# A long convolution with a routed expert layer on one core: the late units' transposes of finished rows move from behind a unit's first step to the unit's head

## The chip, the core and the metric

The kernel runs on one core of a Trainium2 chip. The metric is the time of one execution in microseconds, as the device measures it. The core has TensorE (PE: matrix products and transposes into PSUM; its weight loads are listed apart, as PEld), VectorE (DVE), ScalarE (ACT), GpSimd (POOL, which here also issues the DMAs that gather and scatter rows by a list of indices) and SyncE (SP, which issues plain DMAs). Each engine works through its own list of instructions in the order in which the program wrote them, and semaphores make one engine wait for another.

## The reference

Two layers follow one another. The first is a long convolution of `u = x * v` with a filter, done with Fourier transforms, and a product with `x`:

```python
u = x * v                                   # 4 x 11456 x 128
y = np.fft.irfft(Uf * Hf[None, :, :], n=L, axis=1)[:, :S, :]
return (x * y).astype(np.float32)
```

The second takes the 45,824 rows of that result. A row whose skip score is positive goes through the one of eight experts with the largest logit, and the result, times the expert's gate weight, is added to the row:

```python
h = np.maximum(xc[mask] @ w1[e], 0.0)       # 128 -> 1024
y[mask] = gate_w[mask, None] * (h @ w2[e])  # 1024 -> 128
out[do_compute] = xc + y
```

Rows with a score of zero or less are left as they are.

## The kernel before

The program has four stretches. `first_phase` and `freq_phase` (to about 730 us) compute the convolution's forward transforms and products, `out_phase` (to about 1183 us) transforms back, stores the rows, routes them and already runs a part of the experts' work in between (`early_slots`). What is left of the experts' work runs in `late_slots`, from about 1183 us to the end. The change lies in `late_slots` alone.

`late_slots` works through 36 *units*, `u` = 0 to 35. Units 0 to 28 hold two *slots* each and are called pairs here; units 29 to 31 hold one slot (singles), and units 32 to 35 half a slot (halves). A slot is 256 rows of one expert. For a pair, 512 rows go through these steps:

- **Gather.** `fetch(u + 4)` has POOL gather the rows of the unit four ahead into tiles `xt` (L666), with a short POOL pause behind them (L639).
- **Turning the rows.** `turned(sts(u + 1))` transposes the next unit's rows on PE, four 128x128 transposes (L718) into the PSUM tile `mtp`; ACT copies them to `hl` (L720) and DVE writes what the rounding lost beside it (L724).
- **Going up.** `up` multiplies with the expert's first weights, in four parts `k` = 0 to 3 of six matmuls each (L729 to L731) into a PSUM tile `hp`, of which there are two in turn. `relu` reads `hp` on ACT (L850) and then on DVE (L851) into `hh`.
- **Going down.** `down` multiplies `hh` with the second weights (L862 to L864). It is written as a generator, and `lower()` takes one quarter of it: while unit `u` goes up, the four quarters of unit `u - 1` go down, one behind each part. Behind the last quarter, ACT copies the PSUM tile `my` to `yt` (L868).
- **Turning the results back.** `leave(sts(u - 2), yt.pop(u - 2))` transposes the finished `yt` of the unit two back on PE, four transposes (L875) into the PSUM tile `mto`; DVE multiplies with the gate weight and adds the row (`gated`, L742), and POOL scatters the result into the output (L735), with a pause behind it. The program wraps it in a local function `finish()`.
- **Splitting weights.** `first` and `second` prepare the next unit's first weights and this unit's second ones (ACT L701, DVE L706).

The order is written out by hand, since the stretch is scheduled manually: what the loop over `u` writes first is first on each engine. At the head of a unit the loop writes `fetch` and `turned`. Then the four parts follow, each as `up`, `lower`, `relu` and one step more out of the list `(finish, first, second, nothing)`. So before the change `finish()`, with the transposes L875, stands behind part 0 of a pair. In a single it stands behind part 0 as well, in a half behind `lower()`.

The name `st` holds the gathered rows of each slot and `part(u)` says whether unit `u` is a half.

Of the kernel before, what the change touches and what calls it, by code (L numbers as in the profile page):

```python
# [487 lines left out]
class Experts:  # L488
# [149 lines left out]
    def rest(self):  # L638
        self.nc.gpsimd.memset(self.idle, 0.0)  # L639
# [185 lines left out]
    def late_slots(self, pool):  # L825
# [4 lines left out]
        with (  # L830
# [6 lines left out]
            def turned(sts):  # L837
                return self.turn(sts, pool, mpt.tile([128, 2 * T], F32, name="mtp"))

            def up(w, hl, part):  # L840
                n = hl.shape[2]
                hp = mph.tile([128, 4 * T], F32, name="hp")
                nf = 4 * T // n
                for f in range(nf):
                    self.up(w, hl, hp[:, f * n:(f + 1) * n], part * nf + f)
                return hp

            def relu(hp):
                h = mb.tile([128, 2, 4 * T], F32R, name="hh", bufs=6)
                nc.scalar.activation(h[:, 0], hp, AF.Relu)  # L850
                nc.vector.scalar_tensor_tensor(h[:, 1], hp, 0.0, h[:, 0].bitcast(F32), ALU.max, ALU.subtract)  # L851
                return h

            def down(w2, parts, n):

                y = mpy.tile([128, 2 * T], F32, name="my")[:, 0:n]
                nf = 4 * T // n
                for f in range(F // 128):
                    c = slice(f * D, (f + 1) * D)
                    k = f % nf  # L860
                    h = parts[f // nf][:, :, k * n:(k + 1) * n]
                    nc.tensor.matmul(y, w2[:, 0, c], h[:, 0], start=(f == 0), stop=False)  # L862
                    nc.tensor.matmul(y, w2[:, 0, c], h[:, 1], start=False, stop=False)
                    nc.tensor.matmul(y, w2[:, 1, c], h[:, 0], start=False, stop=(f == F // 128 - 1))  # L864
                    if k == nf - 1 and f < F // 128 - 1:
                        yield
                yt = mb.tile([128, 2 * T], F32, name="yt")[:, 0:n]
                nc.scalar.copy(yt, y)  # L868
                yield yt

            def leave(sts, yt):

                tp = mpt.tile([128, 2 * T], F32, name="mto")
                for j in range(2 * len(sts)):
                    nc.tensor.transpose(tp[:, j * 128:(j + 1) * 128], yt[:, j * 128:(j + 1) * 128], self.ident)  # L875
                for n, (tb, xt, ids, since) in enumerate(sts):
                    o = self.row()
                    for j in range(2):
                        self.gated(o[:, j, 0:D], tp[:, n * T + j * 128:n * T + (j + 1) * 128], xt, j)
                        self.store(o[:, j], ids, j)  # L880
                self.rest()

            def turned_half(st):
                tp = mpt.tile([128, 2 * T], F32, name="mtp")[:, 0:128]
                nc.tensor.transpose(tp, st[1][:, 0, 0:D], self.ident)
                x = pool.tile([128, 2, 2 * T], F32R, name="hl", bufs=2)[:, 0, 0:128].bitcast(F32)
                nc.scalar.copy(x, tp)
                return x

            def weight_half(st, which, p, eng):  # L890
                w = p.tile([128, 2, F], F32R, name=f"ws{which}", bufs=2)[:, 0].bitcast(F32)
                src = (self.w1f, self.w2f)[which][:, ds(self.where(eng, st[0]), F)]
                (eng.copy if eng is nc.scalar else eng.tensor_copy)(w, src)
                return w

            def up_half(w, x):
                hp = mph.tile([128, 4 * T], F32, name="hp")
                for f in range(F // 128):
                    c = slice(f * 128, (f + 1) * 128)
                    nc.tensor.matmul(hp[:, c], w[:, c], x, start=True, stop=True)  # L900
                h = mb.tile([128, 2, 4 * T], F32R, name="hh", bufs=6)[:, 0].bitcast(F32)
                nc.scalar.activation(h, hp, AF.Relu)
                return h

            def down_half(w, h):

                y = mpy.tile([128, 2 * T], F32, name="my")[:, 0:D]
                for f in range(F // 128):
                    c = slice(f * 128, (f + 1) * 128)
                    nc.tensor.matmul(y, h[:, c], w[:, c], start=(f == 0), stop=(f == F // 128 - 1))  # L910
                yield y

            def leave_half(st, y):
                tb, xt, ids, since = st
                o = self.row()
                self.gated(o[:, 0, 0:D], y, xt, 0)
                self.store(o[:, 0], ids, 0)
                self.rest()
# [6 lines left out]
            def fetch(u):  # L925
                if u < count:
                    for n in UNITS[u]:
                        if n not in st:
                            st[n] = self.gather(n, self.listing(n), pool, self.names[n])
                            if n == UNITS[u][-1]:  # L930
                                self.rest()
            for u in range(FETCH):
                fetch(u)
            sts = lambda u: [st[n] for n in UNITS[u]]
            part = lambda u: UNITS[u][0] >= HALF
            w2, yt = {}, {}
            before = iter(())
            for u in range(count + 2):
                fetch(u + FETCH)
                if u + 1 < count:  # L940
                    hl[u + 1] = turned_half(*sts(u + 1)) if part(u + 1) else turned(sts(u + 1))

                def first():
                    if u + 1 < count and part(u + 1):
                        w1[u + 1] = weight_half(*sts(u + 1), 0, pool, nc.scalar)
                    elif u + 1 < count:
                        w1[u + 1] = self.split(st[UNITS[u + 1][0]][0], pool, 0, nc.vector)

                def second():
                    w2[u] = self.split(st[UNITS[u][0]][0], mb, 1, nc.vector)  # L950

                def finish():
                    if u >= 2 and not part(u - 2):
                        leave(sts(u - 2), yt.pop(u - 2))

                def lower():
                    y = next(before, None)
                    if y is not None:
                        yt[u - 1] = y
                        if part(u - 1):  # L960
                            leave_half(*sts(u - 1), y)
                parts = []
                if u >= count:
                    lower()
                    finish()
                elif part(u):
                    w2[u] = weight_half(*sts(u), 1, mb, nc.vector)
                    first()
                    parts = up_half(w1[u], hl[u])
                    lower()  # L970
                    finish()
                elif len(UNITS[u]) == 1:
                    first()
                    hp = up(w1[u], hl[u], 0)
                    finish()
                    parts.append(relu(hp))
                    second()
                    parts.append(relu(up(w1[u], hl[u], 1)))
                else:
                    for k, rest in enumerate((finish, first, second, lambda: None)):  # L980
                        hp = up(w1[u], hl[u], k)
                        lower()
                        parts.append(relu(hp))
                        rest()
                while u >= 1 and u - 1 < count and u - 1 not in yt:
                    lower()
                if u < count:
                    before = down_half(w2[u], parts) if part(u) else down(w2[u], parts, hl[u].shape[2])
                    del w1[u], hl[u]
# [458 lines left out]
```

## Time and profile before

| | us |
|---|---|
| median of 3 timed runs | 1583.29 |
| lowest and highest of them | 1579.92, 1583.38 |
| the profiled execution's own time | 1577.83 |
| its span in the trace | 1576.1 |

The profile is of one execution. Its instructions are listed by engine with their start, their duration and, in square brackets, the time that the engine was idle before and which instruction ended that wait. A matmul's duration is modelled from its start to the last value that it writes, so that matmuls in a row overlap in the list: where they follow each other closely it is the distance between two starts that tells what one costs. Rows of one line that follow each other are merged into one, with "x4" for four. The program's names stand with the result on the left: `mto<-ident,yt` writes `mto` from `ident` and `yt`.

### The profile page before, as it was taken

The numbers are of one execution on the slowest core, as the hardware profiler recorded it, in microseconds if no ns is written. First come the engines' busy times: TensorE is split into PE (matmuls) and PEld (weight loads), VectorE is DVE, ScalarE is ACT, GpSimd is POOL, SyncE is SP. The second block draws the span as 40 slices with busy tenths as digits, with TensorE's granted clock in tenths as the row PEclk, the third lists the DMA queues.
The fourth block names the chain that finished last, engine by engine and source line by source line (L and its number), as shares of the span: only waits on it lengthen the run. The fifth ranks groups of instructions, "written<-read, shape, count | busy, mean of one in ns | idle before, by whom it ended". The sixth has DMA issues, their size and how long they took to land. (4 is left out here: it accounts for less than half of the span.)

```text
span 1576.1 us, 25413 instructions
## 1 busy us (share of the span) xinstructions
PE 1502.5 (95%) x7872; PEld 935.1 (59%) x7872; DVE 1127.8 (72%) x2323; ACT 767.3 (49%) x1637; POOL 1081.1 (69%) x832
## 2 busy tenths in 40 slices
PE   8995999999999999998889999999989999999998
PEld 3552444444444444443457777677767888888888
DVE  2334877888788889996777777776666777777774
ACT  4552545444444544442345554544535555555554
POOL 2013898888888878882166758865777888888756
PEclk9987999999999999998899999999999999999999
DMA  9999999999999979978988778878521111111100
GB/s 318 328 351 338 375 354 366 375 348 335 320 353 331 304 229 290 336 212 275 342 251 291 233 256 262 272 270 252 158 57 37 46 45 47 44 46 44 41 24 29
DMA packets 200382, 361.84 MB, mean 230 GB/s; under 512 B 64588, under 2 KB 140762, under 8 KB 200206
## 3 DMA queue, kind: packets, MB, share of 16 engines
q1 hardware_dynamic: 181078, 316.97, 59.3%
q0 software_dynamic: 16448, 38.88, 8.4%
q10 hardware_dynamic: 2720, 4.34, 0.9%
q8 instruction: 64, 1.05, 0.3%
q14 instruction: 72, 0.59, 0.1%
HBM read 216.70 MB, written 145.42 MB: 230 GB/s over the span
## 5 line engine op out<-in xcount | busy, mean ns | idle before, releaser
L411 PE MATMUL ps<-y,c 128*128 128x512 f32 x720 | 331.3, 596 | 0.3
L479 POOL TENSOR_TENSOR y<-y,p 128x2048 f32<-128x2048 f32 x59 | 267.8, 4540 | 69.0 <-DVE p L400 69.0
L735 POOL DMA_INDIRECT out<-o,ids x182 | 198.5, 1091 | 115.4 <-DVE o L742 77.9
L411 PEld LDWEIGHTS ps<-y,c 128*128 128x128 f32 x720 | 133.4, 190 | 173.0 <-issue 155.7
L666 POOL DMA_INDIRECT xt<-out,ids x182 | 192.5, 1058 | 57.0 <-issue 23.8
L400 DVE TENSOR_TENSOR p<-xp,g 128x1024 f32<-128x1024 f32 x240 | 217.3, 946 | 0.0
L400 DVE TENSOR_TENSOR y<-xp,g 128x1536 f32<-128x1536 f32 x120 | 210.8, 1757 | 4.0
L851 DVE SCALAR_TENSOR_TENSOR hh<-hp,hh 128x1024 fp32r<-128x1024 f32 x122 | 148.7, 1219 | 88.5 <-ACT hh L850 87.2
L412 ACT COPY z<-ps 128x512 f32<-128x512 f32 x180 | 105.6, 586 | 178.3 <-PE ps L411 168.8
L850 ACT ACTIVATE hh<-hp 128x1024 fp32r<-128x1024 f32 x122 | 126.4, 1036 | 88.3 <-PE hp L731 88.3
L480 POOL TENSOR_TENSOR y<-y,p 128x1024 f32<-128x1024 f32 x59 | 139.1, 2358 | 4.6
L1107 PE MATMUL y<-zt,c 128*64 128x512 f32 x384 | 110.8, 650 | 16.6 <-DVE xm L1108 5.1
L639 POOL MEMSET idle<- 128x512 f16 x231 | 126.3, 547 | 0.3
L380 PE MATMUL xp<-x,wf 128*128 128x480 f32 x256 | 115.6, 575 | 11.1 <-DMA x<-x1f 6.7
L209 PE MATMUL ps<-wf,c 60*120 60x384 f32 x512 | 110.9, 528 | 8.0 <-DVE wf L192 8.0
L211 ACT COPY wf<-ps 120x384 f32<-120x384 f32 x256 | 105.3, 493 | 21.2 <-PE ps L209 11.2
L812 PE MATMUL bank<-wd,h 128*128 128x128 f32 x896 | 115.0, 283 | 0.0
L812 PEld LDWEIGHTS bank<-wd,h 128*128 128x128 f32 x896 | 105.1, 193 | 14.6 <-issue 14.0
L192 POOL TENSOR_TENSOR wf<-wf 124x768 f32<-124x768 f32 x45 | 81.9, 1819 | 41.5 <-DVE g L392 31.2
L729 PE MATMUL hp<-hl,ws 128*128 128x512 f32 (+1 forms) x256 | 103.2, 403 | 2.1 <-DVE hh L851 1.4
L383 ACT COPY g<-xp 64x192 f32<-64x192 f32 x120 | 38.0, 316 | 137.4 <-PE xp L380 94.7
L392 DVE TENSOR_TENSOR g<-xp,g 128x128 f32<-128x128 f32 x120 | 34.7, 289 | 97.2 <-ACT g L385 97.0
(199 smaller groups left out, 2925.0 us busy)
## 6 DMA issues: line engine op xcount, KB each, us to landing
wf<-xv SPq DMA_DIRECT2D x64, 768.0 KB
x1d<-wf SPq DMA_DIRECT2D x64, 720.0 KB
x<-x1d SPq DMA_DIRECT2D x60, 768.0 KB
zt<-zd SPq DMA_DIRECT2D x60, 768.0 KB
zd<-z SPq DMA_DIRECT2D x110, 384.0 KB
out<-xm SPq DMA_DIRECT2D x96, 258.0 KB
ox<-xo SPq DMA_DIRECT2D x96, 256.0 KB
x1f<-fx POOLq DMA_DIRECT2D x16, 720.0 KB
```

The source lines that it names most:

```text
L209: nc.tensor.matmul(ps[p], self.c1[rows], u[rows, q * RUN:(q + 1) * RUN], start=True, stop=True)
L380: nc.tensor.matmul(xp[:, k, 0:(NS + NB) * DH], c2(n % PER * KS + j * KH + k), x1[:, j * KH + k], start=True, stop=True)
L400: nc.vector.tensor_tensor(o[:, :, :, j * KH:(j + 1) * KH].rearrange("p s a k b d -> p (s a) k b d"), x[:, None].broadcast_to([128, m, KH, ...
L411: nc.tensor.matmul(zps, c3[:, a, :], y[:, blk, a], start=(a == 0), stop=(a == 1))
L479: nc.gpsimd.tensor_tensor(y[:, 1:], y[:, 1:], p1, ALU.add)
L480: nc.gpsimd.tensor_tensor(y[:, 2:], y[:, 2:], p2, ALU.add)
L639: self.nc.gpsimd.memset(self.idle, 0.0)
L666: ins = nc.gpsimd.indirect_dma_start(out=xt[:, j], out_offset=None, in_=self.rows[0:have], in_offset=bass.IndirectOffsetOnAxis(ap=ids[:, j ...
L735: ins = nc.gpsimd.indirect_dma_start(out=self.rows, out_offset=bass.IndirectOffsetOnAxis(ap=ids[:, j:j + 1], axis=0), in_=o, in_offset=Non ...
L812: nc.tensor.matmul(bank[:, j * D:(j + 1) * D], h[f][:, j * 128:(j + 1) * 128], wd[s][:, f * D:(f + 1) * D], start=(f == 0), stop=(f == F / ...
L850: nc.scalar.activation(h[:, 0], hp, AF.Relu)
L851: nc.vector.scalar_tensor_tensor(h[:, 1], hp, 0.0, h[:, 0].bitcast(F32), ALU.max, ALU.subtract)
```

## The change

The turning back of unit `u - 2` is now written at the head of unit `u`, right behind the turning of unit `u + 1`'s rows. The function `finish` is gone, and what called it now calls nothing:

```diff
                 fetch(u + FETCH)
                 if u + 1 < count:
                     hl[u + 1] = turned_half(*sts(u + 1)) if part(u + 1) else turned(sts(u + 1))
+                if u >= 2 and not part(u - 2):
+                    leave(sts(u - 2), yt.pop(u - 2))
...
-                def finish():
-                    if u >= 2 and not part(u - 2):
-                        leave(sts(u - 2), yt.pop(u - 2))
...
                 if u >= count:
                     lower()
-                    finish()
                 elif part(u):
...
                     lower()
-                    finish()
                 elif len(UNITS[u]) == 1:
                     first()
                     hp = up(w1[u], hl[u], 0)
-                    finish()
                     parts.append(relu(hp))
...
-                    for k, rest in enumerate((finish, first, second, lambda: None)):
+                    for k, rest in enumerate((lambda: None, first, second, lambda: None)):
```

On PE, at the head of unit 3, the difference reads as follows ("+" is now, "-" is before; `mtp` is the turning of the next unit's rows, `mto` the turning back, `hp` part 0 going up):

```order
 L718 MATMUL mtp<-ident,xt_4453 128x128 x2
 L718 MATMUL mtp<-ident,xt_4454 128x128 x2
+L875 MATMUL mto<-ident,yt 128x128 x4
 L729 MATMUL hp<-hl,ws_13155 128x512
 L730 MATMUL hp<-hl,ws_13155 128x512
```

The four transposes of `yt` now stand between the turning of rows and part 0. Their place before, twelve matmuls on in the same unit, behind the first quarter going down (`my`) and ahead of part 1:

```order
 L863 MATMUL my<-hh,ws_13192 128x512
 L864 MATMUL my<-hh,ws_13192 128x512
-L875 MATMUL mto<-ident,yt 128x128 x4
 L729 MATMUL hp<-hl,ws_13155 128x512
 L730 MATMUL hp<-hl,ws_13155 128x512
```

So they moved up over the six matmuls of part 0 and the six of the quarter, to stand with the other four transposes. On PE nothing else moved.

On DVE, behind the writing of `hl` for the next unit, the four `gated` steps (L742) moved over one `relu` step (L851), that of part 0. The piece of the difference:

```order
 L655 COPY tb<-tab 1x1 x2
 L724 TENSOR_TENSOR hl<-mtp,hl 128x512
-L851 SCALAR_TENSOR_TENSOR hh<-hp,hh 128x1024
 L742 SCALAR_TENSOR_TENSOR o_4461<-mto,xt_4447 128x128 x2
 L742 SCALAR_TENSOR_TENSOR o_4458<-mto,xt_4448 128x128 x2
-L851 SCALAR_TENSOR_TENSOR hh<-hp,hh 128x1024
+L851 SCALAR_TENSOR_TENSOR hh<-hp,hh 128x1024 x2
```

So part 0's `relu` on DVE now stands behind the four `gated` steps, beside that of part 1. The order on ACT is the same as before. On POOL it is the same but for one place near the end, where the last single's two scatters now stand ahead of a half's one. No instruction is added or taken away on any engine.

## Rows read from the trace of the kernel before

**Rows 1.** Busy time by engine over the 27 periods from the head of unit 2 to the head of unit 29 (us, number of instructions in brackets, granted clock of TensorE as a share of full speed, DMA share and GB/s).

```profile
1209.23:1528.85 319.62, 319.62 (x1512) 264.20 (x1511) 237.40 (x347) 184.77 (x216) 247.25 (x257) 1.00 0.16 42
```

**Rows 2.** Groups of PE instructions by line in the same stretch: busy us, mean ns of one, and the idle time of PE before them.

```profile
L729 PE MATMUL hp<-hl,ws 128*128 128x512 f32 x216 | 89.1, 413 | 0.0
L718 PE MATMUL mtp<-ident,xt 128*128 128x128 f32 x107 | 16.2, 272 | 0.0
L875 PE MATMUL mto<-ident,yt 128*128 128x128 f32 x108 | 16.1, 272 | 0.0
```

**Rows 3.** The timeline of one pair, PE alone: its head, the place of the turning back, and the next unit's head (start us, duration us).

```profile
1303.79 0.39 PE L864 MATMUL my<-hh,ws 128*128 128x512 f32 x1
1304.02 0.60 PE L718 MATMUL mtp<-ident,xt 128*128 128x128 f32 x4
1304.37 0.48 PE L729 MATMUL hp<-hl,ws 128*128 128x512 f32 x1
1304.69 0.39 PE L730 MATMUL hp<-hl,ws 128*128 128x512 f32 x1
...
1306.97 0.40 PE L864 MATMUL my<-hh,ws 128*128 128x512 f32 x1
1307.20 0.60 PE L875 MATMUL mto<-ident,yt 128*128 128x128 f32 x4
1307.56 0.47 PE L729 MATMUL hp<-hl,ws 128*128 128x512 f32 x1
1307.87 0.40 PE L730 MATMUL hp<-hl,ws 128*128 128x512 f32 x1
...
1310.40 0.39 PE L729 MATMUL hp<-hl,ws 128*128 128x512 f32 x1
...
1315.62 0.40 PE L864 MATMUL my<-hh,ws 128*128 128x512 f32 x1
1315.85 0.60 PE L718 MATMUL mtp<-ident,xt 128*128 128x128 f32 x4
```

**Rows 4.** The same unit's timeline, ACT and DVE.

```profile
1304.22 0.59 ACT L868 COPY yt<-my 128x512 f32<-128x512 f32 x1 [2.12 <-PE my L864]
1304.70 1.03 ACT L850 ACTIVATE hh<-hp 128x1024 fp32r<-128x1024 f32 x1
1305.77 1.23 DVE L851 SCALAR_TENSOR_TENSOR hh<-hp,hh 128x1024 fp32r<-128x1024 f32 x1 [2.22 <-ACT hh L850]
1307.03 0.67 DVE L724 TENSOR_TENSOR hl<-mtp,hl 128x512 fp32r<-128x512 f32 x1
1307.63 1.20 DVE L851 SCALAR_TENSOR_TENSOR hh<-hp,hh 128x1024 fp32r<-128x1024 f32 x1
1308.76 1.11 DVE L742 SCALAR_TENSOR_TENSOR o<-mto,xt 128x128 f32<-128x128 f32 x4
```

**Rows 5.** The timeline at the end of `out_phase`, at one of the 18 places where the weight load of a first transpose (PEld L718) waited for ACT L755.

```profile
1181.90 1.30 ACT L755 ACTIVATE h<-mh 128x512 f32<-128x512 f32 x2 [0.41 <-PE mh L731]
1182.55 0.42 PEld L718 LDWEIGHTS mh<-ident,xt 128*128 128x128 f32 x4 [0.47 <-ACT h L755]
1182.93 1.20 PEld L812 LDWEIGHTS bank<-wd,h 128*128 128x128 f32 x10
1183.04 1.17 PE L812 MATMUL bank<-wd,h 128*128 128x128 f32 x9
```

**Rows 6.** The timeline at unit 29, the first single: PE's wait behind its part 0.

```profile
1531.87 0.39 PE L729 MATMUL hp<-hl,ws 128*128 128x256 f32 x1 [0.76 <-DVE tb L655]
```

**Rows 7.** The timeline at the heads of units 30, 31, 32 and 33, PE and ACT.

```profile
1539.22 0.28 PE L730 MATMUL hp<-hl,ws 128*128 128x256 f32 x1
1539.08 0.59 ACT L868 COPY yt<-my 128x512 f32<-128x512 f32 x1 [4.44 <-PE my L864]
...
1545.51 0.28 PE L730 MATMUL hp<-hl,ws 128*128 128x256 f32 x1
1545.54 0.37 ACT L868 COPY yt<-my 128x256 f32<-128x256 f32 x1 [1.74 <-PE my L864]
...
1551.46 0.94 PE L900 MATMUL hp<-hl,ws 128*128 128x128 f32 x7
1551.89 0.37 ACT L868 COPY yt<-my 128x256 f32<-128x256 f32 x1 [1.76 <-PE mtp L885]
...
1556.45 0.72 PE L900 MATMUL hp<-hl,ws 128*128 128x128 f32 x5
1556.59 0.37 ACT L868 COPY yt<-my 128x256 f32<-128x256 f32 x1 [1.89 <-PE my L864]
```

**Rows 8.** Waits from 1190 to 1530 us: who waited for whom, us in total, times, longest.

```profile
POOL out L735 <- DVE o L742: 22.7, 27, 5.8
```

**Rows 9.** Busy time by stretches (columns as in rows 1), for the granted clock.

```profile
800.00:880.00 80.00, 74.17 (x678) 54.52 (x679) 57.28 (x208) 39.75 (x95) 52.14 (x59) 0.96 0.78 251
880.00:960.00 80.00, 78.61 (x721) 58.51 (x719) 61.05 (x233) 40.59 (x101) 53.59 (x61) 1.00 0.85 270
1040.00:1120.00 80.00, 78.19 (x677) 54.73 (x675) 57.58 (x223) 38.44 (x98) 51.17 (x60) 1.00 0.79 247
1532.00:1560.00 28.00, 28.00 (x217) 26.99 (x218) 18.00 (x29) 16.83 (x23) 18.01 (x20) 1.00 0.11 34
```

**Rows 10.** The timeline of the end: the last matmuls, the last `gated` step and the last scatter.

```profile
1565.70 3.74 PE L910 MATMUL my<-ws,hh 128*128 128x128 f32 x32
1569.48 0.35 DVE L742 SCALAR_TENSOR_TENSOR o<-my,xt 128x128 f32<-128x128 f32 x1 [1.44 <-PE my L910]
1570.11 0.97 POOL L735 DMA_INDIRECT out<-o,ids  x1 [0.27 <-DVEq L991]
```

## The prediction

> **What bounds the kernel now.** I read the busy time by stretch first, then the lines of PE within the stretch, and then one unit in order of time on PE, ACT and DVE.
>
> The change touches `late_slots` alone. From the head of unit 2 to the head of unit 29 the trace has 319.62 us for 27 pairs, and PE is busy in all of it, at a granted clock of 1.00, the 2.4 GHz level [rows 1]. The groups of PE's lines show no idle time ahead of any of them [rows 2]. So a pair takes 319.62 / 27 = 11.84 us. In one unit in order of time, starts of matmuls follow each other at 0.227 us, one after the other, from head to head: 1304.02 to 1315.85 is 11.83 us [rows 3]. ACT, DVE and POOL are busy 185, 237 and 247 us of the 320 [rows 1]. PE bounds this stretch with nothing to spare, and it goes on doing so in the tail: 28.00 of 28 us busy from 1532 to 1560 [rows 9], then matmuls in a row to 1569.44, with the last `gated` step and the last scatter 0.04 and 0.67 us behind them [rows 10]. What PE stands still in `late_slots` lengthens the kernel one for one, unless a wait that it has anyway takes it up.
>
> **The change part by part.**
>
> *The four transposes in a new place.* None is added. Between the matmuls around them, the four of `turned` cost 1304.69 - 1303.79 - 2 x 0.227 = 0.45 us, and the four of `leave` behind part 0 cost 1307.87 - 1306.97 - 2 x 0.227 = 0.45 us [rows 3]. Putting the groups together saves at most a change between the two kinds of work, which the starts do not show as a cost of its own; I take nothing.
>
> *The new wait.* The transposes read `yt`. ACT copies it from 1304.22 to 1304.81, directly behind the last matmul going down, which starts at 1303.79 [rows 3, 4]. Before, the transposes came at 1307.20 and found a copy 2.4 us old. Now they come right behind `turned`, whose four transposes begin at 1304.02 and give the engine away at about 1304.46, and the copy is not done. PE takes its matmuls in order, so the six matmuls of part 0 and everything behind them stand behind this wait, though none of them needs `yt`. What hid the copy was twelve matmuls; what hides it now is four transposes, 0.45 us of the 1.02 us from the last matmul's start to the copy's end.
>
> What that comes to, from start to start: the closest row is the place where transposes L718 waited for ACT. There ACT's pair of activations began at 1181.90 and lasted 1.30, so that the first ended at about 1182.5; the weight load started at 1182.55, 0.05 later; the next matmul's load followed 0.38 and that matmul 0.49 us after it [rows 5]. In the pair, then: load of the first turned-back block at 1304.81 + 0.05 = 1304.86; loads of part 0 from 1305.24; second matmul of part 0 some 0.34 us on (in rows 3 it starts 0.32 behind the first), at 1305.58. Without the wait it would start at 1304.69 + 0.45 = 1305.14. **The stall is 0.45 us a pair.** From below, 0.3 us, if one load of 0.14 us (0.42 for four merged, rows 5) went on beside the wait; from above 0.6 us, if the signal took three times the 0.05 and part 0's first load lay bare too. I take 0.45, since it comes from the nearest row.
>
> *Who feels it behind the wait.* In ACT's list nothing moved; `relu` of part 0 and all behind it come 0.45 us later, with PE. On DVE the four `gated` steps, 1.11 us, now stand ahead of part 0's `relu` [rows 4]. That `relu` frees the PSUM tile which part 2 needs. Before it ended at 1308.83, for a part 2 that starts at 1310.40 [rows 3, 4]. Now `hl` ends at 1307.70, the `gated` steps at about 1308.8, and part 0's `relu` at about 1310.0, while part 2 comes at 1310.40 + 0.45 = 1310.85: still 0.8 us to spare, so no second wait. On POOL the scatters get their rows about 0.6 us earlier against PE, and nobody waits for them in `late_slots` but the end. The moved scatters near the end (two of a single ahead of one of a half) lie well before the last one at 1570.11 [rows 10], which hangs on PE's last matmul; nothing for them.
>
> *The sum.* Units 2 to 28 are pairs with the full cover in front: 27 x 0.45 = 12.2 us (8 to 16 by the bounds). At unit 29 PE already waits 0.76 us behind its part 0, for DVE [rows 6]; the stall comes ahead of that wait and disappears in it: 0. Units 30 to 33 have one or two transposes of `turned` as cover instead of four, and the tail has no such wait. Copy ends are 1539.67, 1545.91, 1552.26 and 1556.96 [rows 7]. Adding 0.05 for the signal, 0.6 (four transposes and the way to the second matmul, 0.38 + 0.02 + 0.20) at unit 30, about 0.39 at unit 31 (two transposes, half of the 0.49 above and a little for the rest, and 0.12 for the matmul behind), 0.27 at the halves, and taking away what the same work would cost without a wait (0.45 for four, 0.225 for two, on the starts 1539.22, 1545.51, 1551.46 and 1556.45), gives 0.65 + 0.6 + 0.9 + 0.6 = 2.75 us. Together **14.9 us more**.
>
> Against the profiled execution's own time, 1577.83 us, this is 1592.7. The timed runs' median lies 5.5 us (0.35%) higher, at 1583.29, and the change is judged by such runs: 1583.29 + 14.9 = **1598 us**, 0.94% slower.
>
> *A rule beside it.* In rows 5 the weight load of the waiting transposes itself started only when the wait ended, 0.47 us idle before it. The Trainium skill, TensorE: Matmul & The Clock Gate, Part 1, Architectural detail, says that PE's queue can pull weight loads ahead of matmuls in flight. By that rule a load of 0.14 us would leave the path at each of 27 waits, and the sum would be 3.8 us smaller, 1594.4; the row speaks against it for a wait of this kind.
>
> **The rivals.**
>
> *Weight loads run ahead of the wait.* The mechanism is that of the lower bound: PE holds the first load of the transposes ready while it waits. For it: the loads of L812 start 0.11 us ahead of their matmuls [rows 5]. Against it: the waiting load in the same rows. 14.9 - 27 x 0.14 = 11.1 us more, 1594 us.
>
> *The stall is taken up.* It would need a wait of PE behind it in each pair, as unit 29 has one. Then the time stays at 1583 us. Against it: 0.0 idle in every group of PE [rows 2]. It could only be if the trace's modelled ends hid waits; but the even 0.227 us between starts leaves no room for 0.45. It decides from 0.3 us of slack a pair on.
>
> *POOL sets the pace, and gets its rows earlier.* This one ends on the other side. POOL's scatters waited 22.7 us in 27 waits for `gated` [rows 8]; if PE's pace came from the gathers behind them in POOL's list, earlier `gated` steps would give back up to that: 1583.3 - 22.7 = 1561 us. It decides if PE waits for `xt` at `turned`. Against it: no idle time ahead of L718 [rows 2], and POOL is busy only 247 of 320 us [rows 1].
>
> *DVE becomes late.* If part 0's `relu` ended 0.8 us later than I reckon, part 2 would wait for its PSUM tile in every pair. At 0.5 us a pair this is 13.5 us on top, 1612 us. It decides where `gated` starts over 0.8 us later than 1307.7. For it: DVE has four kinds of work in a row there without a gap [rows 4].
>
> *The clock drops.* A pair would have PE idle 0.45 of 12.3 us, 3.7%. The granted clock was 1.00 where PE was idle 1.7% and 2.3%, and 0.96 where it was idle 7% [rows 9]. At 0.96, the 27 pairs, 332 us, would take 14 us more: 1612 us. I think 1.00 holds, being nearer.
>
> That the change does not do what it says is excluded: the order of instructions shows the transposes at the head.
>
> **How the numbers follow.** Forecast 0.74 (1598, own range 1591 to 1604 by the bounds of the stall and the difference of the two bases); loads ahead 0.08; taken up 0.08; POOL 0.03; DVE 0.03; clock 0.04. A measurement of this kernel can tell a difference of about 0.3%, 4.8 us. Slower by more than that: 0.74 + 0.08 + 0.03 + 0.04 = 0.89; within it 0.08; faster 0.03. For 8 in 10 the range takes in the forecast with the rival of the loads, and both bases: the lower end is 1577.83 + 11.1 = 1589, the upper end 1583.29 + 27 x 0.6 + 2.75 = 1602, and 3 us for the spread of the runs (1579.92 to 1583.38): 1605.
>
> **What would show it.** Right: the period of a pair grows from 11.84 to about 12.3 us; PE shows a wait on ACT's `yt` copy (L868) ahead of L875, some 0.4 to 0.6 us, at each of units 2 to 28 and 30 to 33, and none at part 2; the granted clock stays 1.00; unit 29's wait for DVE shrinks. Wrong: L875 shows no wait (then the copy came earlier than I read); or a wait ahead of L729 at part 2 with `relu` as its cause (DVE); or a granted clock under 1.00 between 1210 and 1530 us; or a pair at 11.84 us in spite of the wait.

## The result and the profile after

The changed kernel takes 1597.17 us (median of 5 runs, 1592.92 to 1598.81) against 1583.29 us of the kernel before (5 runs, 1578.5 to 1587.34): a ratio of 1.009, 95% interval 1.0072 to 1.0108, so 11 to 17 us slower. The forecast was 1598 us, 14.9 us slower.

The profiled execution took 1598.81 us with a span of 1597.0 us, some 21 us over the span before. Only a part of that belongs to the change. The heads of the units, where the transposes of the next unit's rows begin (L718, L885 for a half), tell it apart: unit 1 begins 6.51 us later (1203.64 against 1197.13 us), in work that the change does not touch; most of it is there early in the first phase, where the first matmul of L380, which waits for a transfer in both kernels, already starts 5.7 us later. The 27 pairs from unit 2 to unit 29 take 11.26 us more, and the stretch from there to the last `gated` step takes 2.86 us more; some 0.35 us comes behind it. So the change costs 11.26 + 2.86 = **14.1 us** in the trace.

The same stretch of 27 pairs as in [rows 1], busy time by engine:

```profile
1215.74:1546.62 330.88, 324.20 (x1511) 264.92 (x1510) 237.37 (x347) 187.45 (x216) 263.07 (x258) 1.00 0.15 41
```

330.88 / 27 = 12.26 us a pair instead of 11.84, at the same granted clock of 1.00. PE is idle in 6.68 us of it, where it was never idle before. The groups of PE's lines in the stretch, as in [rows 2], say ahead of which instruction; the last row is that of the weight loads:

```profile
L729 PE MATMUL hp<-hl,ws 128*128 128x512 f32 x216 | 86.5, 401 | 0.0
L875 PE MATMUL mto<-ident,yt 128*128 128x128 f32 x108 | 17.7, 286 | 6.7 <-ACT yt L868 6.7
L718 PE MATMUL mtp<-ident,xt 128*128 128x128 f32 x107 | 16.2, 272 | 0.0
...
L875 PEld LDWEIGHTS mto<-ident,yt 128*128 128x128 f32 x108 | 11.3, 140 | 13.1 <-ACT yt L868 13.1
```

All of the idle time stands ahead of L875, and ACT's copy L868 ends it. Neither figure is the cost: 6.7 us counts from the modelled end of the matmul ahead, 13.1 us from the end of the load ahead, and the heads moved by 11.26 us. The timeline of one pair shows it from start to start, beside [rows 3, 4]:

```profile
1313.56 0.40 PE L864 MATMUL my<-hh,ws 128*128 128x512 f32 x1
1313.79 0.60 PE L718 MATMUL mtp<-ident,xt 128*128 128x128 f32 x4
1313.99 0.59 ACT L868 COPY yt<-my 128x512 f32<-128x512 f32 x1 [2.12 <-PE my L864]
...
1314.63 0.42 PEld L875 LDWEIGHTS mto<-ident,yt 128*128 128x128 f32 x4 [0.47 <-ACT yt L868]
1314.63 0.66 PE L875 MATMUL mto<-ident,yt 128*128 128x128 f32 x4 [0.24 <-ACT yt L868]
1315.04 0.48 PE L729 MATMUL hp<-hl,ws 128*128 128x512 f32 x1
1315.36 0.39 PE L730 MATMUL hp<-hl,ws 128*128 128x512 f32 x1
1315.54 1.22 DVE L851 SCALAR_TENSOR_TENSOR hh<-hp,hh 128x1024 fp32r<-128x1024 f32 x1 [2.22 <-ACT hh L850]
...
1317.40 1.11 DVE L742 SCALAR_TENSOR_TENSOR o<-mto,xt 128x128 f32<-128x128 f32 x4
...
1317.87 0.39 PE L729 MATMUL hp<-hl,ws 128*128 128x512 f32 x1
...
1318.43 1.21 DVE L851 SCALAR_TENSOR_TENSOR hh<-hp,hh 128x1024 fp32r<-128x1024 f32 x1
```

The copy runs from 1313.99 to 1314.58; the first load of the transposes follows at 1314.63, 0.05 us later, as in [rows 5]; part 0's second matmul starts at 1315.36, 1.80 us behind the last matmul going down. Without a wait it would be 0.90 + 0.45 = 1.35 us [rows 3]. So the wait costs 0.45 us here. Nearly all of it is the copy's lack of cover; some 0.05 us come with the wait itself, since the four transposes last 0.66 us behind it and 0.60 elsewhere. On DVE the `gated` steps stand ahead of part 0's `relu` (1318.43), which now begins 1.0 us later against the head than before, and nobody waits for it: it ends at 1319.64, part 2, which needs the PSUM tile that it frees, starts at 1320.59, and no idle time stands ahead of L729.

### The profile page after: what moved, and what is told of

The parts are those of the page before. It is cut to its first block, busy times and chain, and to the rows that moved or that the text cites. A ratio compares the mean times of both kernels' runs of the same rounds, so it can differ in the third digit from the quotient of the medians.

```text
span 1597.0 us, 25411 instructions
## 1 busy us (share of the span) xinstructions
PE 1510.7 (95%) x7872; PEld 936.4 (59%) x7872; DVE 1128.0 (71%) x2323; ACT 770.9 (48%) x1637; POOL 1095.6 (69%) x832
## 3 DMA queue, kind: packets, MB, share of 16 engines
q8 instruction: 64, 1.05, 0.3%
## 5 line engine op out<-in xcount | busy, mean ns | idle before, releaser
L735 POOL DMA_INDIRECT out<-o,ids x182 | 187.4, 1030 | 114.5 <-DVE o L742 73.4
L666 POOL DMA_INDIRECT xt<-out,ids x182 | 217.9, 1197 | 57.5 <-issue 29.3
L851 DVE SCALAR_TENSOR_TENSOR hh<-hp,hh 128x1024 fp32r<-128x1024 f32 x122 | 148.7, 1219 | 101.4 <-ACT hh L850 101.4
L380 PE MATMUL xp<-x,wf 128*128 128x480 f32 x256 | 117.7, 584 | 8.1 <-DMA x<-x1f 5.8
L706 DVE TENSOR_TENSOR ws<-wf,ws 128x1024 fp32r<-128x1024 f32 x82 | 101.2, 1234 | 2.2 <-issue 1.1
```

Source lines behind the costliest of these rows:

```text
L380: nc.tensor.matmul(xp[:, k, 0:(NS + NB) * DH], c2(n % PER * KS + j * KH + k), x1[:, j * KH + k], start=True, stop=True)
L666: ins = nc.gpsimd.indirect_dma_start(out=xt[:, j], out_offset=None, in_=self.rows[0:have], in_offset=bass.IndirectOffsetOnAxis(ap=ids[:, j ...
L735: ins = nc.gpsimd.indirect_dma_start(out=self.rows, out_offset=bass.IndirectOffsetOnAxis(ap=ids[:, j:j + 1], axis=0), in_=o, in_offset=Non ...
```

## The experiments

Two theories beside the forecast's own, which is that PE, in order, stands behind ACT's copy of `yt`: (A) the new order on DVE (`gated` ahead of part 0's `relu`) costs the time; (B) eight transposes in a row, or the head as a place, cost it, with or without a wait. Later the question was also whether a wait has a price of its own beside its length. The sharp reading in each run is the time of a pair, from head to head, over units 2 to 28; the total time is given with its ratio to the kernel before.

**Turning back behind part 0** (edit to the kernel before):

```diff
                     for k, rest in enumerate((lambda: None, first, second, lambda: None)):
                         hp = up(w1[u], hl[u], k)
+                        if k == 0:
+                            finish()
                         lower()
                         parts.append(relu(hp))
```

> For pairs the whole turning back (transposes, gated, scatter) is written behind part 0 going up but ahead of the first quarter going down and ahead of part 0's relu; singles and halves as in the kernel before. On PE six matmuls (1.36 us) more stand ahead of the transposes than in the changed kernel; on DVE gated stands ahead of part 0's relu exactly as in the changed kernel. Theory (PE stands behind ACT's copy of yt): the copy is 0.4 us old when the transposes come, no wait, a pair takes 11.84 us as before, time within 0.3% of before. Rival (gated ahead of part 0's relu on DVE costs the time): a pair stays at 12.26 us, about 14 us slower than before.

A pair takes (1534.46 - 1215.35) / 27 = 11.82 us; the ratio is 1.0002 (0.9986 to 1.0018). The timeline of one unit has `gated` (L742) ahead of part 0's `relu` (the L851 behind it), as in the changed kernel, and the transposes six matmuls behind the head:

```profile
1309.93 0.60 PE L718 MATMUL mtp<-ident,xt 128*128 128x128 f32 x4
1310.13 0.58 ACT L868 COPY yt<-my 128x512 f32<-128x512 f32 x1 [1.74 <-issue]
1311.68 1.23 DVE L851 SCALAR_TENSOR_TENSOR hh<-hp,hh 128x1024 fp32r<-128x1024 f32 x1 [1.83 <-ACT hh L850]
1311.76 0.60 PE L875 MATMUL mto<-ident,yt 128*128 128x128 f32 x4
1313.54 1.11 DVE L742 SCALAR_TENSOR_TENSOR o<-mto,xt 128x128 f32<-128x128 f32 x4
1314.57 1.20 DVE L851 SCALAR_TENSOR_TENSOR hh<-hp,hh 128x1024 fp32r<-128x1024 f32 x1
```

The order on DVE costs nothing. (A) falls. The copy was 1.05 us old when the transposes came, older than the 0.4 us expected.

**Only the transposes at the head.** `leave` is cut in two; `gated` and the scatter stay where the kernel before has them:

```diff
+                if u >= 2 and not part(u - 2):
+                    back = leave_turn(sts(u - 2), yt.pop(u - 2))
...
-                        leave(sts(u - 2), yt.pop(u - 2))
+                        leave_rows(sts(u - 2), back)
```

> Only the four transposes stand at the head, as in the changed kernel; gated and scatter stay behind part 0, where the kernel before has them. Theory (PE's wait for yt): a pair takes 12.26 us as in the changed kernel, PE waits 0.24 us (0.48 us for its weight load) ahead of the transposes, about 14 us slower than before. Rival (the DVE order costs the time): 11.84 us a pair and no difference from before.

A pair takes 12.26 us, and the ratio is 1.0099 (1.0077 to 1.0122). The timeline of one unit has part 0's `relu` (L851) ahead of `gated`, as in the kernel before, and PE's wait behind the end of the copy:

```profile
1318.83 0.58 ACT L868 COPY yt<-my 128x512 f32<-128x512 f32 x1 [2.12 <-PE my L864]
1319.47 0.66 PE L877 MATMUL mto<-ident,yt 128*128 128x128 f32 x4 [0.24 <-issue]
...
1322.62 1.22 DVE L851 SCALAR_TENSOR_TENSOR hh<-hp,hh 128x1024 fp32r<-128x1024 f32 x1 [0.30 <-ACT hh L850]
1323.76 1.12 DVE L742 SCALAR_TENSOR_TENSOR o<-mto,xt 128x128 f32<-128x128 f32 x4
```

In 23 of the 27 pairs the profile names ACT's copy as what ended PE's wait; in 4, as here, its record of the semaphores has a gap and it says "issue", at the same length and place. Moving four transposes on PE alone brings the whole loss; (A) falls a second time.

**The results of the unit before that, at the head** (the lines that ask for three `yt` buffers and 16 row tiles are left out):

```diff
-                if u >= 2 and not part(u - 2):
-                    leave(sts(u - 2), yt.pop(u - 2))
+                if u >= 3 and not part(u - 3):
+                    leave(sts(u - 3), yt.pop(u - 3))
```

> At the head of unit u the results of unit u - 3 are turned back, not those of u - 2 (three yt buffers, 16 row tiles). Place on PE and order on DVE are those of the changed kernel; the yt read is a whole unit old. Theory (the wait for yt): no wait ahead of the transposes, a pair takes 11.84 us, time within 0.3% of before. Rival (eight transposes in a row, or the head as a place, cost something by themselves, or the clock drops): 12.26 us a pair, some 14 us slower.

The stretch from 1226.52 to 1537.55 us has 26 pairs (the one ahead of it turns nothing back): 24 of 11.77 to 11.81 us, the last of 11.57, and one of 16.59. The ratio is 1.0018 (0.9998 to 1.0038). In a usual unit the two groups of transposes follow each other without a gap:

```profile
1308.75 0.39 PE L864 MATMUL my<-hh,ws 128*128 128x512 f32 x1
1308.98 0.60 PE L718 MATMUL mtp<-ident,xt 128*128 128x128 f32 x4
1309.41 0.60 PE L875 MATMUL mto<-ident,yt 128*128 128x128 f32 x4
1309.77 0.47 PE L729 MATMUL hp<-hl,ws 128*128 128x512 f32 x1
1310.08 0.39 PE L730 MATMUL hp<-hl,ws 128*128 128x512 f32 x1
```

From the last matmul going down to part 0's second matmul it is 1.33 us, where 1.35 was reckoned without a wait. The place and the grouping are free; (B) falls. What is left is the wait for `yt`. The pair of 16.59 us is told of under the last heading.

**One matmul of part 0 ahead of the transposes**, for pairs (the lines that hand the turning back to `up` as `then` are left out):

```diff
         nc.tensor.matmul(hp, w[:, 0, c], hl[:, 0], start=True, stop=False)
+        if then is not None:
+            then()
```

> As the changed kernel, but for pairs the turning back stands behind the first matmul of part 0: 0.227 us more cover on PE. Theory (the stall is what the copy lacks in cover): the stall falls from 0.42 to about 0.19 us, a pair takes about 12.03 us, 5.2 + 2.85 = 8 us slower than before. Rival (a wait costs a fixed restart of PE, whatever its length): a pair stays near 12.26 us. Rival (DVE order): 12.26 us as well, with no wait shown.

A pair takes 12.04 us, as expected: 0.227 us of cover takes 0.22 us off the loss. The total came out higher, a ratio of 1.0078 (1.0054 to 1.0103): the profile's unit 31 takes 10.39 us instead of the changed kernel's 6.70, and ACT is idle 3.69 us ahead of its copy of `yt` there, with nothing of this core named as the cause (1.48 us in the changed kernel). So 2.2 us of the unit's 3.69 us more are ACT's longer wait; behind it the granted clock was 0.50, the 1.2 GHz level, for 3.4 us, and the rest came with that. The timeline of one pair:

```profile
1312.42 0.59 ACT L870 COPY yt<-my 128x512 f32<-128x512 f32 x1 [2.12 <-PE my L866]
1312.58 0.47 PE L729 MATMUL hp<-hl,ws 128*128 128x512 f32 x1
1313.06 0.42 PEld L877 LDWEIGHTS mto<-ident,yt 128*128 128x128 f32 x4 [0.32 <-ACT yt L870]
1313.07 0.66 PE L877 MATMUL mto<-ident,yt 128*128 128x128 f32 x4
1313.48 0.47 PE L732 MATMUL hp<-hl,ws 128*128 128x512 f32 x1
```

PE shows no idle time at all here, because the matmul ahead is modelled to last until the transposes begin; in the 27 pairs it is busy 324.61 of 324.96 us and still 0.2 us a pair too slow. A stall shorter than a matmul's modelled length is seen only from start to start, or on the weight load.

**The copy made twice:**

```diff
                 nc.scalar.copy(yt, y)
+                nc.scalar.copy(yt, y)
```

> As the changed kernel, but ACT makes its copy of yt twice, so that the second ends about 0.55 us later; the values are the same. Theory (PE stands behind the copy): the stall grows by the second copy's length, 0.5 to 0.59 us, to about 0.97 us; a pair takes about 12.8 us, 27 x 0.97 + 5 = some 31 us slower than before. Rival (ACT's copy is not what PE waits for): 12.26 us a pair. If the clock falls with longer waits, the granted clock falls under 1.00 and a pair takes more than 13 us.

A pair takes 12.85 us, 0.60 more than the changed kernel: the second copy starts 0.61 us behind the first, and PE follows it one for one. The granted clock stays 1.00 with a gap of 0.86 us in each pair:

```profile
1316.33 0.60 PE L718 MATMUL mtp<-ident,xt 128*128 128x128 f32 x4
1316.53 0.59 ACT L868 COPY yt<-my 128x512 f32<-128x512 f32 x1 [2.12 <-PE my L864]
1317.14 0.59 ACT L869 COPY yt<-my 128x512 f32<-128x512 f32 x1
1317.78 0.31 PEld L876 LDWEIGHTS mto<-ident,yt 128*128 128x128 f32 x3 [1.09 <-ACT yt L869]
1317.78 0.44 PE L876 MATMUL mto<-ident,yt 128*128 128x128 f32 x2 [0.86 <-ACT yt L869]
```

The ratio, 1.0122 (1.0063 to 1.0181), is less than the pairs say. In the runs measured together with this one and those below, the kernel before has a median of 1598 us itself, not 1583: the versions with the copy twice or shared and the one with the head from unit 29 on ran on another chip, the last two versions on the first chip again, at a later time. The last heading says what can be seen of that.

**The copy shared by ACT and DVE:**

```diff
-                nc.scalar.copy(yt, y)
+                nc.scalar.copy(yt[:, 0:h], y[:, 0:h])
+                nc.vector.tensor_copy(yt[:, h:n], y[:, h:n])
```

> As the changed kernel, but ACT copies one half of yt and DVE the other at the same time (DVE is idle 2.2 us there). Theory: a half takes ACT 0.37 us (the row of 256 columns) and DVE about 0.4, so yt is ready about 0.2 us earlier; the stall falls from 0.42 to about 0.23 us, a pair takes about 12.05 us, some 6 to 9 us slower than before. Rival (restart of fixed cost): a pair stays at 12.26 us. DVE's 0.4 us more work costs nothing in the pairs, since DVE idles there.

This missed: a pair takes 12.29 us, no less than the changed kernel (ratio 1.0023, 0.9998 to 1.0048). The two halves did not run side by side. DVE's half starts when ACT's has ended:

```profile
1311.21 0.37 ACT L869 COPY yt<-my 128x256 f32<-128x256 f32 x1 [2.12 <-PE my L864]
...
1311.62 0.42 DVE L870 COPY yt<-my 128x256 f32<-128x256 f32 x1 [1.07 <-ACT yt L869]
1311.64 0.20 PEld L877 LDWEIGHTS mto<-ident,yt 128*128 128x128 f32 x2 [0.26 <-ACT yt L869]
...
1312.09 0.20 PEld L877 LDWEIGHTS mto<-ident,yt 128*128 128x128 f32 x2 [0.26 <-DVE yt L870]
```

So `yt` was ready 0.83 us behind the copy's start instead of 0.59, while two transposes went ahead of that. The program itself asks for that order: in the trace DVE's copy carries a wait for the semaphore that ACT's instructions raise, and it starts 0.03 us behind the end of ACT's half in every pair. The run does not speak against the theory, but it is no test of half a copy, and it does not show that the two engines could not have copied side by side.

**The copy in two halves on ACT:**

```diff
-                nc.scalar.copy(yt, y)
+                nc.scalar.copy(yt[:, 0:h], y[:, 0:h])
+                nc.scalar.copy(yt[:, h:n], y[:, h:n])
```

> As the changed kernel, but ACT copies yt in two halves, one behind the other, so that the first two transposes wait for the first half alone and the last two for the second. By the row of 256 columns a half takes 0.37 us, and the next instruction of ACT starts about 0.1 us before the one ahead of it ends, so the second half ends about 0.65 us after the first began (0.59 in one piece). Theory (PE stands behind the end of the copy, in order): the first pair of transposes goes at +0.42 instead of +0.64 us behind the copy's start and lies beside the second half; the second pair goes at about +0.70; behind it two transposes remain instead of four, so part 0 comes about 0.16 us earlier, a pair takes 12.1 us, and the tail is 0.5 us shorter. Rival (a wait costs a fixed restart of PE, now paid twice): 12.3 us or more.

All but four pairs take 12.08 to 12.12 us; two take 17.64 and 17.69, with a pair of 12.2 or 12.15 behind each. The ratio is 1.0056 (1.0033 to 1.0078). The timeline of one pair:

```profile
1314.40 0.37 ACT L869 COPY yt<-my 128x256 f32<-128x256 f32 x1 [1.88 <-issue]
1314.67 0.38 ACT L870 COPY yt<-my 128x256 f32<-128x256 f32 x1
1314.83 0.71 PE L877 MATMUL mto<-ident,yt 128*128 128x128 f32 x4
1315.30 0.48 PE L729 MATMUL hp<-hl,ws 128*128 128x512 f32 x1
```

Two waits instead of one, and a pair is 0.14 us shorter: what a wait costs is in the main what the data lack. A fixed price of the size of the loss is excluded, one of some 0.05 us a wait is not (the four transposes last 0.71 us here, 0.66 behind one wait and 0.60 behind none).

**The head from unit 29 on only.** Pairs keep the place of the kernel before:

```diff
+                pair = u < count and len(UNITS[u]) == 2
+                if not pair:
+                    back()
```

> The turning back stands at the head only from unit 29 on (three singles, four halves); pairs as in the kernel before. Theory: a pair takes 11.84 us; unit 29 takes 10.03 us in both kernels, since its stall disappears in the wait for DVE that stands behind it; from the head of unit 29 to the last gated step 40.63 us become 43.5 us, 0.7 + 0.6 + 0.9 + 0.6 us at units 30 to 33. Rival (the tail's length comes from the pairs' later scatters, or from POOL): 40.6 us as before.

Unit 29 takes 10.03 us, as in both kernels. Units 30 to 33 take 7.09, 10.40, 5.89 and 4.52 us, where the changed kernel has 7.09, 6.70, 5.90 and 4.52 and the one before 6.40, 6.08, 4.98 and 3.90. But for unit 31, where ACT is idle 3.89 us ahead of its copy, these are the tail's terms without any change in the pairs, so the tail's loss is its own. The single execution took 1609.2 us.

**The older results at the head, and part 3's relu ahead of the copy on ACT** (beside the edits of the run with older results):

```diff
+                        if k == 3:
+                            parts.append(relu(hp))
                         lower()
-                        parts.append(relu(hp))
+                        if k < 3:
+                            parts.append(relu(hp))
```

> The results of unit u - 3 are turned back at the head (as in one_older), and part 3's relu goes ahead of the copy of yt on ACT. Theory: no wait for yt; eight transposes in a row cost 0.055 us less than four and four, as one_older's pairs of 11.78 us show, so a pair takes 11.78 us; unit 29's wait of 0.76 us behind its part 0 goes, since DVE gets part 3's relu earlier, so unit 29 takes 9.3 us instead of 10.03. Together 1.5 + 0.8 = 2.3 us less than before, 0.15%, which a measurement of this kernel cannot tell from no change; the trace can. Rival (the wait at unit 29 is not for part 3's relu): 10.03 us.

Usual pairs take 11.77 to 11.81 us and unit 29 takes 9.00 us, 0.3 less than expected and 1.03 less than before: its wait behind part 0 was for part 3's `relu`, late on ACT behind the copy. The wait is worth more than the 0.76 us of idle time in [rows 6], because that counts from the modelled end of the transposes ahead: they start at 1530.51 there and the next matmul at 1531.87, 1.36 us later, where 0.36 us is usual [rows 3]. The total does not show it (ratio 1.0011, 0.9981 to 1.0041), since eight pairs of this profile took 12.45 to 19.14 us. No version measurably beats the kernel before.

## Why the prediction was right

*What bounds it.* PE was busy without a gap, and every stall of PE lengthened the kernel one for one: heads, pairs and total agree, 14.1 us in the trace and 11 to 17 us in the runs.

*The new wait.* It is the whole cause. It is there when the transposes alone are moved, and gone when the data are older or six matmuls stand ahead. Its size follows what the copy lacks in cover: 0.42 us in the changed kernel, 0.20 with one matmul more of cover, 0.27 with the copy in halves, 1.02 with the copy twice, against 11.84 us.

*Its size.* The step from the last matmul going down to part 0's second one was reckoned at 1.79 us and is 1.80 (1.79 makes a stall of 0.44 us, which the prediction rounds to 0.45). A pair grew by 0.42 us on average and not 0.45, which makes 11.3 us and not 12.2 in 27 pairs. Two departures are in that average. Units 2 to 27 grew by 0.41 us each: behind the old place of the transposes the matmuls start 0.230 us apart, elsewhere in the unit 0.227 or 0.228 [rows 3], and that 0.03 to 0.04 us a pair went with them. What makes them so was not tested. Unit 28 grew by 0.64 us, from 11.62 to 12.26. The prediction gave it the full cover, but at its head the rows of unit 29 are turned, a single, with two transposes and not four; the 107 instructions of L718 beside the 108 of L875 in [rows 2] could have told. So 26 x 0.04 us less and 0.2 us more make the 0.9 us between 12.2 and 11.3. The forecast's own range of 1591 to 1604 us does not come out of its bounds: with the tail's 2.75 us, 0.3 to 0.6 us a pair make 10.9 to 19.0 us, so 1594 to 1602 us from the median.

*Unit 29 and the tail.* Unit 29 takes 10.03 us before and after: its stall vanished in the wait that it had (0.76 us idle before, 0.10 after). Units 30 to 33 grew by 0.69, 0.62, 0.92 and 0.62 us, 2.85 together, for 0.65, 0.6, 0.9 and 0.6 reckoned.

*The rivals.* The first load of the waiting transposes starts 0.05 us behind the copy, so the loads did not run ahead of the wait, and the pairs came out at 12.26 us, not the 12.15 of that rival. In the trace the wait for ACT's semaphore is marked on that load itself, ahead of the matmul, in all 27 pairs. The rule of the Trainium skill (TensorE: Matmul & The Clock Gate, Part 1, Architectural detail), that PE's queue can pull weight loads ahead of matmuls in flight, shows no effect at a load that waits itself, by the 1314.63 us row, and is not refuted by it either. The sign named for the wait, 0.4 to 0.6 us ahead of L875, is met by the load's idle time (0.47); the matmul's row shows 0.24. The stall was not taken up. POOL's earlier rows gave nothing back. DVE had room for the `gated` steps, 0.95 us of it. The granted clock stayed 1.00.

## What to carry to other kernels

An instruction on an engine that has no idle time is best placed where its inputs are old: what counts is the work that stands between the end of its producer and itself on its own engine, and here 0.45 us of transposes did not cover a copy that ends 1.02 us behind the last matmul, while six matmuls more did. Grouping like work is worth nothing by itself if it brings a consumer next to its producer. A stall of that size may not show as idle time at all; compare the starts of the same instruction from one round of the loop to the next.

## What else the runs showed

**ACT's work comes late at times, and the cause is open.** In the pair of 16.59 us of the run with older results, ACT had nothing in hand for 6.16 us and PE came to wait 3.10 us for it:

```profile
1436.85 1.02 ACT L850 ACTIVATE hh<-hp 128x1024 fp32r<-128x1024 f32 x1 [6.16 <-remote]
...
1439.18 0.79 PE L729 MATMUL hp<-hl,ws 128*128 128x512 f32 x1 [3.10 <-DVE hh L851]
1439.77 0.63 PE L730 MATMUL hp<-hl,ws 128*128 128x512 f32 x1
1440.20 0.63 PE L731 MATMUL hp<-hl,ws 128*128 128x512 f32 x1
```

The `relu` at 1436.85 is part 1's, whose matmuls had ended at about 1432.0 us. The profile names nothing of this core ("remote"), but the trace's record of semaphores tells more: ACT starts 0.02 us behind a rise of the semaphore that PE's matmuls raise, as elsewhere, and that rise comes 4.8 us behind the end of the last part 1 matmul, where 0.01 to 0.02 us is usual, while PE's next matmuls went on at their usual pace. At unit 31 of the run with one matmul ahead it is the same, 2.2 us late. So it is the signal from PE that came late, not ACT that lingered. The record has gaps in these profiles, so this is read from the rises that it does have. Such waits are in one pair in the four profiles of the first group of runs, and in several pairs of three of the five later profiles: the 27 pairs of the run with the head from unit 29 on, which are as in the kernel before, take 336.80 us there instead of 319.62, and the last two versions, on the first chip again, have them as well. So they do not belong to one chip. Five profiles have one of 2.95 to 3.89 us at unit 31 (1.48 in the changed kernel's), where PE, with the transposes at the head, stands behind it. If the kernel before had such waits in the later runs too, which no profile of it shows, its 1598 us hold some of them, and the ratios say less than the pairs. What delays the signal is open, and so is why the runs with the copy twice or shared have none in their pairs.

**After a wait of 3.1 us TensorE ran at its lower level; after 0.86 us it did not.** Granted clock (the column behind POOL) in the windows around the wait above:

```profile
1436.00:1439.20 3.20, 0.10 (x2) 0.02 (x1) 1.29 (x2) 1.96 (x2) 2.64 (x4) 0.94 0.14 44
1439.20:1442.00 2.80, 2.80 (x7) 2.22 (x8) 1.06 (x1) 0.83 (x1) 2.50 (x2) 0.50 0.18 41
1442.00:1460.00 18.00, 18.00 (x88) 15.03 (x87) 14.16 (x24) 11.11 (x14) 12.31 (x13) 0.99 0.14 34
```

In the window of 2.8 us the clock was 0.50, the 1.2 GHz level, and matmuls started 0.43 us apart instead of 0.227. In the same way it fell to 0.50 at unit 31 of the run with one matmul ahead, where PE had been idle 2.61 us, and it stayed at 1.00 at unit 31 of the run with the copy twice, where PE had been idle 2.27 us. The stalls of the changed kernel never came near that.
